# Block 0 with another order of loads, and the spills of the first four filter spectra moved into the down projection

## The chip, the cores and the metric

The kernel runs on one core of a Trainium2 chip. The metric is device time in microseconds of one launch; the median of three runs of the kernel before is 561.41 us (558.75 to 562.42). The profile of the kernel before is of one such run, with a span of 556.9 us from its first to its last instruction. The engines are called as the profile calls them: PE (matmul), DVE (vector), ACT (scalar), POOL (GpSimd) and SP, whose queue issues nearly all the DMA transfers.

## The reference, cut to what matters

A block with conditioning has two halves: a gated long convolution along the sequence, and a gated feed-forward layer. All tensors are bfloat16; S = 2048 rows, D = 576 columns, F = 4608.

```python
mod = (silu(c) @ w_mod).reshape(1, 6, 1, -1)         # w_mod: 576 x 3456
sa, ca, ga, sb, cb, gb = (mod[:, i] for i in range(6))

h = layernorm(q) * (1 + ca) + sa
k_shift = sum over t of k[t - j] * shift_k[:, j]      # 4 taps
kv = k_shift * v
y = irfft(rfft(kv padded) * rfft(ssm_k padded))[:S] + kv * ssm_D
x = q + ga * (h * y)

h2 = layernorm(x) * (1 + cb) + sb
out = x + gb * ((silu(h2 @ w1) * (h2 @ w3)) @ w2)
```

The long convolution is causal: row s of y needs all rows of kv up to s, and the filter ssm_k at the same distances.

## The kernel before

The 2048 rows are cut into eight blocks of 256 rows for the convolution and four groups of 512 rows for the feed-forward layer. Each block s has a spectrum X[s] of its kv rows and a spectrum V[s] of its stretch of the filter (both are 128 x 3456 in bfloat16, 864 KB). Block s of the output is the sum over j of X[j] * V[s-j], so later blocks use earlier spectra again. Only three X and four V fit on chip; the others are written to DRAM (`Xd`, `Vd`) and read back.

The feed-forward layer of group r runs on PE while the convolution of the next two blocks (a Python generator, advanced a little after each piece) uses DVE, ACT and the gaps of PE. A scheduler puts the instructions after block 1 in order, engine by engine; in block 0 the order of PE, DVE and ACT is that of the program text.

The start of the kernel, and block 0:

```python
    def early_loads(self):
        nc = self.nc
        self.crow = self.hp.tile([1, D], BF16, name="crow", tag="sg")
        self.shk_raw = self.prod.tile([1, 4 * D], BF16, name="shk_raw", tag="p")
        nc.scalar.dma_start(self.shk_raw[:], self.shift_k.rearrange("d j -> (d j)").rearrange("(o n) -> o n", o=1))
        def between():
            self.load_k(0)                           # ssm_k, block 0 -> knat
            nc.sync.dma_start(self.crow[:], self.c)
            self.load_x(0)                           # q, block 0
        self.load_kv(0, between)                     # k with its halo -> kh, and v -> vt; one row of kh on ACT's queue
        nc.scalar.dma_start(self.drow[0:4, :], self.ssm_D[0:512].rearrange("(a p) -> a p", p=P))
        nc.scalar.dma_start(self.drow[4:5, 0:64], self.ssm_D[512:D].rearrange("(o p) -> o p", o=1))
        self.load_mod(0, 3)                          # w_mod for sa, ca, ga: 1.9 MB
        self.load_mod(3, 2)                          # w_mod for sb, cb: 1.3 MB

    def first_block(self):
        ...
        self.angles(nc.vector, 1)
        self.whole_turns(1)
        self.whole_turns(0)
        self.shift_taps()                            # PE spreads shift_k over the partitions; ACT, DVE copy it
        self.waves(1)                                # ACT: sine table Fk, for the filter
        self.waves(0)                                # ACT: sine table Fb, for the kv rows
        self.warm(4)                                 # four matmuls without use, to keep PE busy
        ...
        self.cond_silu()
        pt = self.ps((P, 2, 1024), BF16)
        nc.tensor.transpose(pt[:, 0, 0:5], self.drow[:], self.ident[0:5, 0:5])
        nc.scalar.copy(self.dcol[:], pt[:, 0, 0:5])  # ssm_D as a column
        tap = self.knat[:, :, 0]
        nc.gpsimd.tensor_add(tap, tap, self.dcol[:]) # ssm_D is added to the filter's tap 0
        self.run_all(self.k_rows(0))                 # PE transposes knat, ACT copies it: kT
        self.load_k(1)
        self.warm(4)
        rows = self.kv_rows(0)                       # DVE: shifted k times v
        self.cond()                                  # PE, ACT: silu(c) over the partitions: crep
        self.run_all(self.w_spectrum(0))             # PE: 16 matmuls on Fk, ACT: 4 copies -> W
        self.run_all(rows)
        mean, rstd = self.quick_stats(x1[:, 1, :], "l1")
        ...
        self.run_all(self.x_spectrum(0))             # PE: 16 matmuls on Fb, ACT: 4 copies -> X
        self.run_all(self.v_block(0))                # DVE: V from W
        ...                                          # loads of w1, w3; products X*V; mod_piece(2), (1), (0) on crep
        ps = [self.inverse(0, cc) for cc in range(2)]
        self.run_all(self.gate(0))
        self.run_all(self.k_rows(1))
        self.mod_columns()
        pt = [self.ps((P, 2, 1024), BF16) for _ in range(2)]
        self.residual_row(0, 0, ps[0])
        st = [self.quick_stats(x1[:, 0, :], "l2")]
        self.residual_row(0, 1, ps[1])
        self.normed(0, 0, *st[0])
        self.turn_split(pt[0], 0)                    # PE transposes half 0 of h2
        self.turned_split(pt[0], 0, False)           # ACT: five pieces into h2T
        st.append(self.quick_stats(x1[:, 1, :], "l2"))
        self.normed(0, 1, *st[1])
        self.turn_split(pt[1], 1)
        self.turned_split(pt[1], 1, True)            # ACT: three pieces, DVE: two
        ...
```

The spectra and their spills, and the two phases of a group of 512 rows:

```python
    def x_sums(self, s):
        ...
        if 1 < s < NBLK - 2:
            self.keep_x(s)                           # X[s] -> Xd, on SP's queue

    def v_block(self, s):
        ...
        self.V[s] = V
        if 1 < s < NBLK - 1:
            self.keep_v(s)                           # V[s] -> Vd, on SP's queue
        yield 0.75

    def down(self, r, rate):                         # h @ w2
        nc = self.nc
        for h in range(2):
            accs = [self.ps() for _ in range(2)]
            for f0 in range(0, NF, W2C):
                w = self.w2p.tile([P, W2C, H], BF16, name="w2t", tag="w2t")     # 4 buffers
                nc.sync.dma_start(w[:], ...)
                ...
                for f, t in order:
                    nc.tensor.matmul(...)
                self.advance(rate * W2C * 4 * 0.126)

    def row_blocks(self, n1):                        # n1 = 6
        ...
            if r == 0:
                for fc in (n1 - 2, n1 - 1):
                    self.hidden(0, fc, 256, 512, rate, self.kept[fc])
                for fc in range(n1, NF // FC):       # weight pieces 6, 7, 8
                    self.hidden(0, fc, 0, RB, rate)
                    if fc - n1 < 2:
                        self.keep_x(fc - n1)
                        self.keep_v(fc - n1)
                for fc in range(n1 - 2):             # pieces 0 to 3 again, for rows 256 to 511
                    self.hidden(0, fc, 256, 512, rate)
            ...
            self.down(r, rate)
```

A weight piece (`wst`) is 128 columns times 4 of w1 and of w3, 1152 KB in four transfers, and has two buffers. Before this loop, the rows of block 0 alone (256) have gone through pieces 0 to 5 while the convolution of block 1 ran.

Of the kernel before, what the change touches and what calls it, by code (L numbers as in the profile page):

```python
# [9 lines left out]
BF16 = mybir.dt.bfloat16  # L10
# [5 lines left out]
P = 128  # L16
S = 2048
D = 576
F = 4608
B = 256  # L20
NBLK = S // B
# [6 lines left out]
W2C = 4  # L28
# [13 lines left out]
class _Kernel:  # L42
# [28 lines left out]
    def setup(self):  # L71
# [3 lines left out]
        self.npi = const.tile([P, 1], F32, name="npi")  # L75
        self.neghalf = const.tile([P, 2], F32, name="neghalf")
        self.shk = const.tile([P, 4, D], BF16, name="shk")
        self.drow = const.tile([5, P], BF16, name="drow")
        self.dcol = const.tile([P, 5], BF16, name="dcol")
        self.h3 = const.tile([P, NF, RB], BF16, name="h3")  # L80
        self.wm = self.h3[:].rearrange("p a b -> p (a b)")
# [23 lines left out]
        nc.vector.memset(self.neghalf[:], -0.5)  # L105
        self.one = self.small.tile([1, P], BF16, name="one", tag="one", bufs=1)
        nc.vector.memset(self.one[:], 1.0)
        nc.vector.memset(self.drow[:], 0.0)
        self.ang = {}
        self.angles(nc.gpsimd, 0)  # L110
        make_identity(nc, self.ident[:])
# [3 lines left out]
    def early_loads(self):  # L115
        nc = self.nc
        self.crow = self.hp.tile([1, D], BF16, name="crow", tag="sg")
        self.shk_raw = self.prod.tile([1, 4 * D], BF16, name="shk_raw", tag="p")
        nc.scalar.dma_start(self.shk_raw[:], self.shift_k.rearrange("d j -> (d j)").rearrange("(o n) -> o n", o=1))
        def between():  # L120
            self.load_k(0)
            nc.sync.dma_start(self.crow[:], self.c)
            self.load_x(0)
        self.load_kv(0, between)
        nc.scalar.dma_start(self.drow[0:4, :], self.ssm_D[0:512].rearrange("(a p) -> a p", p=P))
        nc.scalar.dma_start(self.drow[4:5, 0:64], self.ssm_D[512:D].rearrange("(o p) -> o p", o=1))
        self.load_mod(0, 3)
        self.load_mod(3, 2)

    def load_mod(self, m, n):  # L130

# [217 lines left out]
    def v_block(self, s):  # L349

        nc = self.nc
        W = self.Wl[s]
        V = self.spec.tile([P, 6, D], BF16, name="V", tag="V")
        if s == 0:
            nc.vector.tensor_copy(V[:, 0:6:3, :], W[:, 0:4:2, :])
            VS = W[:, 1:4:2, :]
        else:
            Wp = self.Wl[s - 1]
            nc.vector.tensor_add(V[:, 0:5:4, :], W[:, 0:4:3, :], Wp[:, 1:3, :])
            nc.vector.tensor_sub(V[:, 1:4:2, :], W[:, 1:3, :], Wp[:, 0:4:3, :])  # L360
            VS = V[:, 1:6:3, :]
        nc.vector.tensor_add(V[:, 2:6:3, :], V[:, 0:6:3, :], VS)
        yield 2.25
        nc.vector.tensor_sub(V[:, 1:6:3, :], VS, V[:, 0:6:3, :])
        self.V[s] = V
        if 1 < s < NBLK - 1:
            self.keep_v(s)
        yield 0.75

# [203 lines left out]
    def first_block(self):  # L573
# [5 lines left out]
        self.whole_turns(1)  # L579
        self.whole_turns(0)  # L580
        self.shift_taps()
        self.waves(1)
        self.waves(0)
        self.warm(4)
        sums = [self.small.tile([P, 1], F32, name="l1" + k, tag="sr" + k) for k in "um"]
        self.cond_silu()

        pt = self.ps((P, 2, 1024), BF16)
        nc.tensor.transpose(pt[:, 0, 0:5], self.drow[:], self.ident[0:5, 0:5])
        nc.scalar.copy(self.dcol[:], pt[:, 0, 0:5])  # L590
        tap = self.knat[:, :, 0]
        nc.gpsimd.tensor_add(tap, tap, self.dcol[:])
        self.run_all(self.k_rows(0))
        self.load_k(1)
        self.warm(4)
        rows = self.kv_rows(0)
        self.cond()
        self.run_all(self.w_spectrum(0))
        self.run_all(rows)
        mean, rstd = self.quick_stats(x1[:, 1, :], "l1")  # L600
        nmr = self.small.tile([P, 1], F32, name="l1nm", tag="nmr1")
# [30 lines left out]
        self.residual_row(0, 0, ps[0])  # L632
        st = [self.quick_stats(x1[:, 0, :], "l2")]
        self.residual_row(0, 1, ps[1])
        self.normed(0, 0, *st[0])
        self.turn_split(pt[0], 0)
        self.turned_split(pt[0], 0, False)
        st.append(self.quick_stats(x1[:, 1, :], "l2"))
        self.normed(0, 1, *st[1])
        self.turn_split(pt[1], 1)  # L640
        self.turned_split(pt[1], 1, True)
        W1 = self.w_spectrum(1)
# [186 lines left out]
    def down(self, r, rate):  # L829
# [4 lines that stand above are left out]
                w = self.w2p.tile([P, W2C, H], BF16, name="w2t", tag="w2t")  # L834
                nc.sync.dma_start(w[:], self.w2[f0 * P:(f0 + W2C) * P, h * H:(h + 1) * H]
                                  .rearrange("(a p) d -> p a d", p=P))
                last = f0 + W2C == NF
                order = [(f, t) for f in range(W2C) for t in range(4)]
                if last:
                    order = [(f, t) for t in range(4) for f in range(W2C)]  # L840
                for f, t in order:
                    nc.tensor.matmul(accs[t // 2][:, t % 2, 0:H],  # L842
                                     self.h3[:, f0 + f, t * P:(t + 1) * P], w[:, f, :],
                                     start=(f0 + f == 0), stop=(f0 + f == NF - 1))
                self.advance(rate * W2C * 4 * 0.126)
            for t in range(4):
                s, cc = 2 * r + t // 2, t % 2
# [32 lines left out]
    def row_blocks(self, n1):  # L880
        for r in range(NRB):
# [7 lines left out]
            if r == 0:  # L889
# [3 lines left out]
                for fc in range(n1, NF // FC):  # L893
                    self.hidden(0, fc, 0, RB, rate)
                    if fc - n1 < 2:
                        self.keep_x(fc - n1)
                        self.keep_v(fc - n1)
                for fc in range(n1 - 2):
                    self.hidden(0, fc, 256, 512, rate)
            else:  # L900
# [57 lines left out]
```

## Time and profile before

| what | number |
|---|---|
| median of three runs | 561.41 us (558.75 to 562.42) |
| span of the profiled run | 556.9 us |
| PE busy | 525.7 us (94%) |
| DVE busy | 316.6 us (57%) |
| ACT busy | 303.8 us (55%) |
| bytes moved by DMA | 119.29 MB, mean 214 GB/s |
| block 0, from 0 to 38.4 us: PE busy | 27.75 us |
| from 84 to 110 us: PE busy, DMA | 26.00 us, 327 GB/s |
| from 110 to 137 us: PE busy, DMA | 23.50 us, 321 GB/s |

PE is the busiest engine by far, so what the time can lose is PE's idle time, and what a change can add is work or waits on PE. Nearly all idle time of PE lies in three places: block 0, the stretch from 119 to 137 us (the end of the hidden phase of the first group) and around 172 us (the end of its down phase). From 190 us on PE stands still only for fractions of a microsecond at a time.

A line of the timeline has the start and the busy time of an instruction or a run of equal ones, the engine (PE; PEld for weight loads; a q after the name for the engine's queue, which issues transfers), the line of the kernel, the operation, the output and inputs, and in square brackets how long the engine had stood idle and what ended that. A line of the windows has the stretch, its length, the busy time and number of instructions of each engine, the granted clock of PE as a share of full speed, the mean busy share of the sixteen DMA engines, and GB/s.

### The profile page before, as it was taken

How to read it: one execution, taken by the hardware profiler on the slowest of the kernel's cores; microseconds unless marked ns; L12 is line 12 of the kernel's file. 1: busy time of each engine (PE TensorE's matmuls, PEld its weight loads, DVE VectorE, ACT ScalarE, POOL GpSimd, SP SyncE). 2: the span in 40 equal slices, each digit the busy share in tenths (PEclk: the TensorE clock that was granted, in tenths of full speed). 3: DMA queues.
4: the chain of work that ended last, by engine and by line, in shares of the span. 5: the costliest groups of instructions: out<-in, count | busy, mean ns of one | idle time of the engine just before them, and what ended most of it. 6: DMA issues, size and time to landing. Idle time of an engine off the chain costs nothing.

```text
span 556.9 us, 9033 instructions
## 1 busy us (share of the span) xinstructions
PE 525.7 (94%) x3495; PEld 305.0 (55%) x3495; DVE 316.6 (57%) x486; ACT 303.8 (55%) x638; POOL 45.5 (8%) x111
## 2 busy tenths in 40 slices
PE   5969989997997999999999999989999999999996
PEld 2656665444775644434477744334478733333775
DVE  8679656696884268595894259979442121222011
ACT  4658686956924166848915165675955055555100
POOL 3202010202102000101101000030201000000000
PEclk9979989998999999999999999999999999999999
DMA  8953689998898677966897679654264545432352
GB/s 246 288 158 110 218 299 298 333 341 263 300 314 267 186 264 228 340 225 197 292 326 250 179 239 353 202 164 153 89 184 123 148 143 167 143 121 77 99 154 88
DMA packets 103206, 119.29 MB, mean 214 GB/s; under 512 B 5179, under 2 KB 93308, under 8 KB 103164
## 3 DMA queue, kind: packets, MB, share of 16 engines
q1 hardware_dynamic: 103150, 118.72, 67.8%
q8 instruction: 27, 0.44, 0.3%
q14 instruction: 15, 0.12, 0.1%
q10 hardware_dynamic: 14, 0.01, 0.0%
HBM read 104.84 MB, written 13.86 MB: 213 GB/s over the span
## 4 chain that ended last, share of the span: by engine, by line
PE 66%; ACT 10%; DVE 10%; DMA 7%; issue 3%; POOL 3%; SPq 0%; ACTq 0%; DVEq 0%
PE ps L801 32%; PE ps L842 19%; PE ps L809 5%; PE ps L288 4%; ACT junk L401 4%; DMA wst<-in_B_w_dram 3%; DVE p L380 3%; DMA X<-Xd 2%; DVE z L382 2%; PE ps L485 2%; ACT h2row L513 1%; ACT sg L815 1%; DMA V<-Vd 1%; ACT X L291 1%; PE ps L518 1%
## 5 line engine op out<-in xcount | busy, mean ns | idle before, releaser
L801 PE MATMUL ps<-h2T,wst 128*128 128x512 bf16 (+1 forms) x1344 | 272.4, 352 | 5.7 <-DMA wst<-in_B_w_dram 4.1
L801 PEld LDWEIGHTS <-wst 128*128 128x128 bf16 x1344 | 126.5, 99 | 133.5 <-issue 24.1
L815 ACT ACTIVATE sg<-ps 128x512 bf16<-128x512 f32 (+1 forms) x168 | 91.3, 543 | 150.0 <-PE ps L809 90.0
L842 PE MATMUL ps<-w2t,h 128*128 128x288 bf16 x1152 | 143.6, 286 | 0.9 <-DMA w2t<-in_B_w_dram 0.8
L842 PEld LDWEIGHTS <-h 128*128 128x128 bf16 x1152 | 112.3, 98 | 29.9 <-DMA w2t<-in_B_w_dram 1.5
L818 DVE TENSOR_TENSOR h<-sg,u 128x512 bf16<-128x512 bf16 (+1 forms) x168 | 63.5, 383 | 110.6 <-ACT u L817 110.3
L817 ACT CAST u<-ps 128x512 bf16<-128x512 f32 (+1 forms) x168 | 88.6, 527 | 0.8 <-DVE h L818 0.8
L850 DVE TENSOR_TENSOR og<-ps,gbrow 128x288 bf16<-128x288 f32 x32 | 13.1, 449 | 82.6 <-PE ps L842 82.6
L380 DVE TENSOR_TENSOR p<-X,V 128x3456 bf16<-128x3456 bf16 x28 | 54.6, 1951 | 4.2 <-DMA X<-Xd 3.9
L382 DVE TENSOR_TENSOR z<-z,p 128x3456 bf16<-128x3456 bf16 x28 | 54.6, 1950 | 0.1
L809 PE MATMUL ps<-h2T,wst 64*128 64x512 bf16 (+1 forms) x336 | 46.7, 352 | 0.5 <-ACT X L291 0.5
L401 ACT ACTIVATE junk<-x 128x576 bf16<-128x576 bf16 x58 | 40.0, 689 | 12.9 <-DVE x L501 12.3
L416 POOL TENSOR_SCALAR l1m<-l1s 128x2 f32<-128x2 f32 x7 | 7.8, 1110 | 241.8 <-ACT junk L401 241.8
L809 PEld LDWEIGHTS <-wst 64*128 64x128 bf16 x336 | 9.8, 94 | 31.9 <-issue 30.6
L288 PE MATMUL ps<-kv,Fb 128*128 128x288 bf16 x128 | 19.5, 291 | 3.8 <-ACT u L817 2.3
L681 ACT CAST y<-ps 128x576 bf16<-128x576 f32 x14 | 8.9, 643 | 22.2 <-PE ps L485 22.2
L288 PE MATMUL ps<-kT,Fk 128*128 128x288 bf16 x128 | 20.8, 316 | 0.0
L513 ACT ACTIVATE h2row<-x,l2n,l2r 128x576 bf16<-128x576 bf16 (+1 forms) x28 | 16.2, 671 | 7.5 <-POOL l2n L421 7.5
L291 ACT CAST W<-ps 128x576 bf16<-128x576 f32 x32 | 19.2, 662 | 1.6 <-PE ps L288 1.5
L291 ACT CAST X<-ps 128x576 bf16<-128x576 f32 x32 | 18.9, 661 | 0.3 <-PE ps L288 0.3
L288 PEld LDWEIGHTS <-Fb 128*128 128x128 bf16 x128 | 12.2, 100 | 12.1 <-issue 6.7
L308 DVE TENSOR_TENSOR kv<-kv,kvt 128x1152 bf16<-128x1152 bf16 x24 | 18.0, 752 | 0.3
(115 smaller groups left out, 327.7 us busy)
## 6 DMA issues: line engine op xcount, KB each, us to landing
wst<-in_B_w_dram SPq DMA_DIRECT2D x80, 512.0 KB, 5.3
w2t<-in_B_w_dram SPq DMA_DIRECT2D x72, 288.0 KB, 3.1
X<-Xd SPq DMA_DIRECT2D x12, 864.0 KB, 7.7
V<-Vd SPq DMA_DIRECT2D x10, 864.0 KB, 8.4
Vd<-V SPq DMA_DIRECT2D x7, 864.0 KB, 4.7
Xd<-X SPq DMA_DIRECT2D x6, 864.0 KB
wst<-in_B_w_dram SPq DMA_DIRECT2D x80, 64.0 KB, 3.6
kh<-in_A_k_dram SPq DMA_DIRECT2D x7, 720.0 KB, 6.1
```

Of the source, the lines that this page charges most:

```text
L288: nc.tensor.matmul(ps[:, h, 0:H], basis[:, cc, cs, e, :], rhs[:, cc, h * H:(h + 1) * H], start=(cc == 0), stop=(cc == 1))
L291: nc.scalar.copy(dst(e, cs).rearrange("p (h d) -> p h d", h=2), ps[:, :, 0:H])
L380: nc.vector.tensor_mul(p[:], X[:], V[:])
L382: nc.vector.tensor_add(z[:], z[:], p[:])
L401: self.nc.scalar.activation(junk[:], src[:, i, :], func, accum_out=out[:, col:col + 1])
L513: self.nc.scalar.activation(row[:, cc, at:at + hi - lo], x1[:, cc, lo:hi], ACT.Identity, bias=b[:, cc:cc + 1], scale=r[:, cc:cc + 1])
L801: nc.tensor.matmul(gus[fi][:, i, 0:n], w[:, 5 * i + ct, fi * P:(fi + 1) * P], hT[:, ct, t0:t1], start=(first and ct == 0), stop=(not first ...
L809: nc.tensor.matmul(gus[fi][:, i, 0:n], w[rows, 4, fi * P:(fi + 1) * P], hT[rows, 4, t0:t1], start=first, stop=not first)
L815: nc.scalar.activation(sg[:, 0:n], gus[fi][:, 0, 0:n], ACT.Silu)
L817: nc.scalar.copy(u[:, 0:n], gus[fi][:, 1, 0:n])
L818: nc.vector.tensor_mul(self.h3[:, f, t0:t1], sg[:, 0:n], u[:, 0:n])
L842: nc.tensor.matmul(accs[t // 2][:, t % 2, 0:H], self.h3[:, f0 + f, t * P:(t + 1) * P], w[:, f, :], start=(f0 + f == 0), stop=(f0 + f == NF ...
```

## The change: what it does and what it is for

Three parts.

The first is block 0. ssm_D is loaded in one transfer at the head of ACT's queue, is turned by two small matmuls right after the taps, and is added to the filter before the sine tables are made; the filter's rows are turned next, and silu(c) and its spreading over the partitions (`cond`) come after them, `cond` after the matmuls of the filter's spectrum. One matmul without use fewer stands ahead of them. The load of w_mod for sb and cb, and the next block's filter, are held back until DVE has done three of the four taps: a one-element write into the destination makes the transfer wait. This is to let the transfers that block 0 needs first go alone, and to take ACT's and PE's work in the order in which the path needs it.

The second is the end of block 0: the statistics of the second half of the rows are taken before the first half is normalised, and DVE takes two of the five pieces of both halves of h2T.

The third moves the spills of V[0] to V[3] out of the hidden phase of the first group into its down phase, four of them spread over the loads of w2.

```diff
@@ setup, early_loads
-        self.drow = const.tile([5, P], BF16, name="drow")
+        self.drow = const.tile([9, 64], BF16, name="drow")
...
-        nc.vector.memset(self.drow[:], 0.0)
+        nc.vector.memset(self.dcol[:], 0.0)
...
+        nc.scalar.dma_start(self.drow[:], self.ssm_D.rearrange("(a p) -> a p", p=64))
         nc.scalar.dma_start(self.shk_raw[:], ...)
...
         self.load_kv(0, between)
-        nc.scalar.dma_start(self.drow[0:4, :], self.ssm_D[0:512].rearrange("(a p) -> a p", p=P))
-        nc.scalar.dma_start(self.drow[4:5, 0:64], self.ssm_D[512:D].rearrange("(o p) -> o p", o=1))
         self.load_mod(0, 3)
-        self.load_mod(3, 2)
@@ v_block
-        if 1 < s < NBLK - 1:
+        if 3 < s < NBLK - 1:
             self.keep_v(s)
@@ first_block
         self.shift_taps()
+        ps = self.ps()
+        nc.tensor.matmul(ps[0:64, 0, 0:5], self.drow[:], self.ident[0:9, 0:9:2], start=True, stop=True)
+        nc.tensor.matmul(ps[64:P, 0, 0:4], self.drow[:], self.ident[0:9, 1:9:2], start=True, stop=True)
+        nc.scalar.copy(self.dcol[:, 0:4], ps[:, 0, 0:4])
+        nc.scalar.copy(self.dcol[0:64, 4:5], ps[0:64, 0, 4:5])
+        tap = self.knat[:, :, 0]
+        nc.gpsimd.tensor_add(tap, tap, self.dcol[:])
         self.waves(1)
         self.waves(0)
-        self.warm(4)
+        self.warm(3)
         sums = ...
+        self.run_all(self.k_rows(0))
         self.cond_silu()
-
-        pt = self.ps((P, 2, 1024), BF16)
-        nc.tensor.transpose(pt[:, 0, 0:5], self.drow[:], self.ident[0:5, 0:5])
-        nc.scalar.copy(self.dcol[:], pt[:, 0, 0:5])
-        tap = self.knat[:, :, 0]
-        nc.gpsimd.tensor_add(tap, tap, self.dcol[:])
-        self.run_all(self.k_rows(0))
-        self.load_k(1)
         self.warm(4)
         rows = self.kv_rows(0)
+        for _ in range(3):
+            next(rows)
+        nc.vector.memset(self.wm[0:1, 3 * D:3 * D + 1], 0.0)
+        self.load_mod(3, 2)
+        self.load_k(1)
+        self.run_all(self.w_spectrum(0))
         self.cond()
-        self.run_all(self.w_spectrum(0))
         self.run_all(rows)
...
         self.residual_row(0, 1, ps[1])
+        st.append(self.quick_stats(x1[:, 1, :], "l2"))
         self.normed(0, 0, *st[0])
         self.turn_split(pt[0], 0)
-        self.turned_split(pt[0], 0, False)
-        st.append(self.quick_stats(x1[:, 1, :], "l2"))
         self.normed(0, 1, *st[1])
+        self.turned_split(pt[0], 0, True)
         self.turn_split(pt[1], 1)
@@ down
                     nc.tensor.matmul(...)
+                if r == 0 and (f0 // W2C) % 4 == 3:
+                    self.keep_v(2 * h + f0 // (4 * W2C))
                 self.advance(rate * W2C * 4 * 0.126)
@@ row_blocks
                     if fc - n1 < 2:
                         self.keep_x(fc - n1)
-                        self.keep_v(fc - n1)
```

The program text says where a spill is meant to stand, but the scheduler orders SP's queue by what is ready. In the built program the four spills stand ahead of the down phase: V[0] and V[1] around the load of weight piece 8, V[2] between the two halves of the next load of piece 0, V[3] after the spill of X[2] and just ahead of the next load of piece 1. The first three loads of w2 stand earlier than before, after the load of piece 7. The readback of V[3] stands where it stood, behind the load of piece 1. On DVE, PE and ACT nothing of note is moved after block 0.

## The prediction

> **What bounds the kernel now.** I read the page's busy times first, then its slices, to see where PE falls short, since PE is busy 94% of the span.
>
> ```profile
> PE 525.7 (94%) x3495; PEld 305.0 (55%) x3495; DVE 316.6 (57%) x486; ACT 303.8 (55%) x638; POOL 45.5 (8%) x111
> ...
> PE   5969989997997999999999999989999999999996
> ...
> DMA  8953689998898677966897679654264545432352
> ```
>
> PE's idle time is 556.9 - 525.7 = 31 us, most of it in the first third; DMA stands at 8 to 9 there too. The windows by stage say how much is at stake where the change acts.
>
> ```profile
> 0.00:38.40 38.40, 27.75 (x196) 17.41 (x197) 28.47 (x58) 20.42 (x37) 9.97 (x27) 0.92 0.88 250
> ...
> 84.00:110.00 26.00, 26.00 (x169) 13.79 (x168) 16.91 (x26) 20.44 (x43) 3.61 (x6) 1.00 0.99 327
> 110.00:137.00 27.00, 23.50 (x163) 13.27 (x161) 24.30 (x34) 16.66 (x42) 2.99 (x6) 0.96 1.01 321
> ```
>
> Block 0 is a chain of single steps, no engine's throughput. From 84 to 137 us the DMA engines are full (shares 0.99 and 1.01) at 321 to 327 GB/s: a byte added there has to be paid. PE feels it only in the second half, where it waits for weights; the timeline of PE has these two:
>
> ```profile
> 124.11 0.61 PE L801 MATMUL ps<-h2T,wst 128*128 128x256 bf16 x4 [0.59 <-DMA wst<-in_B_w_dram]
> ...
> 134.65 0.93 PE L801 MATMUL ps<-h2T,wst 128*128 128x256 bf16 x4 [1.47 <-DMA wst<-in_B_w_dram]
> ```
>
> For block 0 I followed the timeline of all engines:
>
> ```profile
> 5.47 0.23 ACTq L126 DMA_DIRECT2D drow<-in_A_ssm_D_dram  x1
> 5.74 1.29 ACT L182 CAST shk<-ps 128x1024 bf16<-128x1024 f32 x2 [3.74 <-DVE ang L160]
> ...
> 9.80 0.35 POOL L592 TENSOR_TENSOR knat<-knat,dcol 128x5 bf16<-128x5 bf16 x1 [3.87 <-ACT dcol L590]
> ...
> 10.20 1.25 PE L336 MATMUL ps<-ident,knat 128*128 128x128 bf16 x10 [1.90 <-POOL knat L592]
> ...
> 11.49 1.12 ACT L338 COPY kT<-ps 128x1152 bf16<-128x1152 bf16 x1 [1.77 <-PE ps L336]
> ...
> 13.87 4.02 PE L288 MATMUL ps<-kT,Fk 128*128 128x288 bf16 x16
> ```
>
> The filter's matmuls cannot start before 13.87 because the tap waits for ssm_D, and ssm_D for the second of its two transfers, whose issue sits in ACT's stream: ACT stops until 5.47, and only then copies the taps, though PE had begun them at 2.90. Sine tables, silu and the ssm_D copy follow in that order.
>
> **What the Trainium skill says.** "TensorE: Matmul & The Clock Gate", section on the architecture, says ACT and DVE are strict FIFO; the ACT lines above agree: nothing passes the blocked issue. Its part on the HAM clock gate says that a busy window of about 3.4 us, free-running, doubles PE's clock and an idle one halves it. The trace agrees in kind: the 16 filter matmuls take 4.02/16 = 0.25 us each, the later ones of the same width 0.13, and the granted clock falls to 0.5 after PE's pause from 30.7 to 33.5. "DMA: Bandwidth & Descriptors", section on queues, rings and completion order, says descriptors on a ring are consumed in order. I checked that with bytes: from the load of weight piece 6 (issued 82.8) to that of piece 1 (landed 124.1) the queue holds 12.5 MB, which at 326 GB/s is 38.5 us; counted from 84 it ends at 122.5, so landing comes 1.6 us behind. The queue is FIFO to that accuracy.
>
> **Block 0, step by step.** One more issue ahead of the taps' load (0.26 us for the small one, up to 0.5) moves the taps on PE from 2.90 to about 3.4 and their end from 4.97 to 5.4. ACT, no longer blocked, copies the last taps by 5.95 instead of 7.03. Two ssm_D copies of 0.14 to 0.2 us: 6.3. The filter landed at about 6.45, so POOL's add (0.35) ends at 6.85 rather than 10.15. PE is in three idle matmuls of 0.43 us until 7.3, transposes until 8.55 (1.25), and four more idle matmuls until 10.3 (1.7). ACT makes Fk and Fb from 6.3 to 8.5, kT until 9.65. So the filter's matmuls start at 10.3, not 13.87: 3.6 us earlier. They end at 14.3 (4.02), the last W copy at 15.0. Here some is given back: `cond`'s two copies (0.59 + 0.26) now stand on ACT between W and X, so X's copies start at 15.9 against 18.88: 3.0 us. DVE's product chain then starts at 17.05 against 20.09. PE's mod pieces start at about 17.3 rather than 20.16; they need w_mod, whose last part landed at 19.0 in the trace. By 17.8 about 4.4 MB had been moved, while the transfers up to and with the first part of w_mod are 3.6 MB, a sum reached at about 15. With the second part held back I expect landing at 15 to 16.5, just in time. ACT's sums for the layer norm, behind ga, start at 19.5 against 22.24: 2.75 us, and POOL, hg and the residual follow at that distance. I take 2.9.
>
> The end of block 0: the pieces of h2T are ACT 5, ACT 3, DVE 2 before; ACT 3, DVE 2, ACT 3, DVE 2 after. The second half's statistics (0.82 + 0.21 + 0.15 us) move ahead of the first half's normalising (0.63), so the first transposes come 1.3 us later and the second 0.4 earlier, and the last DVE pieces end at 38.6 against 38.5 on the old clock. Worth nothing: 0 to 0.2. Sum for block 0: **-2.9 us** (-1.5 to -4). As PE is full or waits on its own buffers after it, all of it should reach the end.
>
> **The spills.** Each is 864 KB, 0.885 MB, or 2.7 us of the full queue. Before they were issued so:
>
> ```profile
> 71.68 0.43 SPq L389 DMA_DIRECT2D Vd<-V  x1
> ...
> 89.67 0.35 SPq L389 DMA_DIRECT2D Vd<-V  x1
> ...
> 95.75 6.65 SPq L389 DMA_DIRECT2D Vd<-V  x2
> ```
>
> In the built order V[0] moves from 71.7 into the full stretch (+2.7 us). In exchange the next block's k (0.74 MB, 2.3 us) moves out of it: it stood behind piece 6 and now stands ahead, at about 79.4, while DMA is at 0.49 and 0.16 of its time from 80 to 84. Three w2 loads go to about 94. Queue by queue at 326 GB/s on the old clock: piece 6, v and X[1] done at 91.2; piece 7 at 94.4; filter and w2 at 98.2; V[0] 102.2; piece 8 at 105.4; V[1] 108.1; V[2] 111.7; piece 0 at 115.3; X[2] 118.0; V[3] 120.7; piece 1 at 124.4. Landing 1.7 later is 126.1 against 124.07, a wait 2 us longer. But piece 2 is the wait that counts next: readback of V[3], k, v and it end at 133.9, landed 135.8 instead of 134.86. So the two waits are not added: PE is **+1 us** later at 136 (0 to +3). Behind that DMA falls idle in both. The down phase gets no spill, so it doesn't gain; it keeps its own wait on the block's convolution:
>
> ```profile
> 172.41 0.56 PE L518 MATMUL ps<-ident,h2row 128*128 128x128 bf16 x5 [2.00 <-ACT h2row L513]
> ```
>
> That is a chain on DVE behind a readback of X, whose order is unchanged. **Sum:** -2.9 + 1.0 = -1.9 us, or 559.5 from the median; as the four times known (558.6, 558.75, 561.4, 562.4) average 560.3, I say 558.8.
>
> **Rivals.** (1) The full queue is the bound after all: V[0] costs its 2.7 us and the readback of V[3], which must now wait for its own spill, blocks SP and all weights behind it. For it: shares of 1.0 for 52 us. Against: k moves out, and V[3] lands at about 122.4, before the next k would be issued (123.7) anyway. Time: 561 to 563. (2) w_mod becomes the wait of block 0: held to 19.0, PE's mod pieces gain 1 us instead of 2.9, and the time is 560.5. Against: 0.8 MB leaves the queue ahead of it. (3) PE's clock rises one window earlier, as the idle matmuls now run without a pause into the filter's: up to 2 us more in the filter's and X's matmuls, though copies of 0.64 us a group then bind. Time: 557.
>
> **Range and chances.** Run to run the kernel spreads over 3.7 us; block 0 is uncertain by 1.3, the spills by 1.5. Together: 555.5 to 562.3. Two percent are 11 us, more than all the idle time of block 0, so faster by that has 0.02; slower 0.02, if weights are blocked repeatedly; 0.96 within.
>
> **What would show it.** Right: ACT's taps at 4.2 without the queue's block, the first filter matmul at 10.3, hidden matmuls from 35.5 instead of 38.4, the waits on weights near 121 to 133 one or two us longer. Wrong: mod pieces waiting for w_mod; SP blocked at V[3]'s readback beyond 124; new waits of PE between 84 and 119.

## The result, and the profile after

The changed kernel takes 554.64 us (median of four runs, 553.28 to 554.84) against 560.33 us of the kernel before beside it (558.75 to 562.42): a ratio of 0.9891, 95% interval 0.985 to 0.9932. Twenty more runs of the same program in a later series gave 556.5 us (551.18 to 561.61) against 560.15 us, a ratio of 0.9925 [0.9898, 0.9953]. The change is worth about 4 us, perhaps somewhat more, and the first four runs lay on the lucky side of its spread. I had predicted 558.8 us and a range from 555.5 to 562.3; the first measurement fell below it by 0.9 us, while the median of the twenty later runs lies inside it.

The page of the changed kernel: its busy times, then its slices.

```profile
PE 520.8 (94%) x3495; PEld 302.5 (55%) x3495; DVE 317.3 (57%) x489; ACT 302.9 (55%) x637; POOL 46.8 (8%) x111
...
PE   6888899997988999999998999989899999999996
...
PEclk9969999999999999999999999999999999999999
DMA  8935789998996686976996689553364535432452
```

And the clock's line from the page of the kernel before, which was not shown yet:

```profile
PEclk9979989998999999999999999999999999999999
```

The span fell by 4.0 us (556.9 to 552.9), and PE's busy time fell by 4.9 us (525.7 to 520.8) with the same number of matmuls, 3495. PE's idle time, which the change was to shorten and which I had counted, did not fall over the whole span: 31.2 to 32.1 us. Equal work took PE less time, and the clock's lines say how: before, slices 3, 6 and 10 are below full speed, after, only slice 3. The later two of before need not be the change's doing: the second profile of the changed kernel has slices of this kind as well.

The windows put most of this in block 0. Each stretch ends with the first hidden matmul of its kernel. The columns are those of the windows of before: stretch, length, busy time and count of PE, then of its weight loads, DVE, ACT and POOL, the granted clock, DMA's share, GB/s. Before:

```profile
0.00:38.40 38.40, 27.75 (x196) 17.41 (x197) 28.47 (x58) 20.42 (x37) 9.97 (x27) 0.92 0.88 250
```

After:

```profile
0.00:33.53 33.53, 24.48 (x196) 16.23 (x197) 28.79 (x60) 19.29 (x36) 10.73 (x27) 0.89 0.93 287
...
84.00:110.00 26.00, 26.00 (x155) 12.42 (x154) 18.16 (x27) 20.30 (x41) 3.61 (x6) 1.00 1.01 332
110.00:137.00 27.00, 23.29 (x179) 14.66 (x178) 21.10 (x31) 18.14 (x51) 4.80 (x12) 1.00 0.91 305
```

The hidden matmuls start 4.87 us earlier. The same 196 matmuls were busy 3.27 us less (27.75 - 24.48), and PE's idle time fell by 1.60 us (10.65 to 9.05). From 84 to 110 us PE is as full as before (26.00 us), so no new waits arose there. The granted clock in this view can't be read for the first microseconds: it shows full speed until its first recorded event, at 18.7 us before and 9.1 us after, though the matmuls ahead of it run at half speed. The durations of equal matmuls are the safer reading. The timeline of the changed kernel, with start and busy time first:

```profile
0.75 0.60 ACTq L119 DMA_DIRECT2D drow<-in_A_ssm_D_dram  x1
...
4.95 1.44 ACT L180 CAST shk<-ps 128x1024 bf16<-128x1024 f32 x2 [2.95 <-PE ps L173]
...
6.29 0.17 ACT L584 CAST dcol<-ps 128x4 bf16<-128x4 f32 x1
...
6.81 0.21 POOL L587 TENSOR_TENSOR knat<-knat,dcol 128x5 bf16<-128x5 bf16 x1 [0.94 <-DMA knat<-in_A_ssm_k_dram]
...
7.31 1.27 PE L334 MATMUL ps<-ident,knat 128*128 128x128 bf16 x10
8.38 1.40 PE L569 MATMUL ps<-h2T,ident 128*128 128x512 bf16 x4
9.79 2.12 PE L286 MATMUL ps<-kT,Fk 128*128 128x288 bf16 x16
...
12.56 0.76 DVE L308 TENSOR_TENSOR kv<-kv,vt 128x1152 bf16<-128x1152 bf16 x1
...
13.09 0.29 ACT L199 CAST crep<-ps 64x128 bf16<-64x128 f32 x1
...
13.37 1.83 PEld L286 LDWEIGHTS <-Fb 128*128 128x128 bf16 x16 [1.10 <-DVE kv L308]
13.37 2.13 PE L286 MATMUL ps<-kv,Fb 128*128 128x288 bf16 x16 [0.96 <-ACT crep L199]
15.34 4.36 PE L208 MATMUL ps<-h,crep 128*128 128x288 bf16 x30
```

The two lines of the kernel before that answer to the last two, from the same view:

```profile
17.68 2.65 PE L288 MATMUL ps<-kv,Fb 128*128 128x288 bf16 x16
20.16 4.36 PE L210 MATMUL ps<-h,crep 128*128 128x288 bf16 x30
```

The chain of ssm_D is as planned: the add waits for the filter's own load and nothing else, and the modulation's matmuls (L208) wait for no load of w_mod. The sixteen filter matmuls, however, take 2.12 us and not 4.02: PE ran them at the full clock. Not all of that is won: X's matmuls, next on PE but for `cond`, wait 0.96 us. Their line names ACT's copy of `crep`, but that copy ends at 13.38, after they have begun; the weight load beside them names DVE's product kv, which ends at 13.32, and the second profile of the changed kernel names kv for the matmuls too (0.85 us). So DVE is what X waits for once the filter's matmuls are fast.

The waits on weight pieces at the end of the first hidden phase, after:

```profile
120.20 0.61 PE L806 MATMUL ps<-h2T,wst 128*128 128x256 bf16 x4 [0.78 <-DMA wst<-in_B_w_dram]
...
127.33 0.61 PE L806 MATMUL ps<-h2T,wst 128*128 128x256 bf16 x4 [1.07 <-DMA wst<-in_B_w_dram]
...
130.20 0.61 PE L806 MATMUL ps<-h2T,wst 128*128 128x256 bf16 x4 [1.29 <-DMA wst<-in_B_w_dram]
```

They fall about 4 us earlier than the three of before (124.11, 131.61, 134.65), and their sum is 3.1 us against 3.5. The prediction showed two of those three and left out the one between them:

```profile
131.61 0.61 PE L801 MATMUL ps<-h2T,wst 128*128 128x256 bf16 x4 [1.44 <-ACT junk L401]
```

The profile puts it down to ACT, but the weights of these matmuls landed at 131.56, just as that ACT instruction ended, and a second profile of the same kernel has this wait at 131.43, put down to the weights.

The moved spills were issued so:

```profile
94.21 0.49 SPq L387 DMA_DIRECT2D Vd<-V  x1
...
97.30 0.66 SPq L387 DMA_DIRECT2D Vd<-V  x1
...
103.85 0.54 SPq L387 DMA_DIRECT2D Vd<-V  x1
...
109.51 1.47 SPq L387 DMA_DIRECT2D Vd<-V  x1
...
116.54 0.34 SPq L392 DMA_DIRECT2D V<-Vd  x1
```

The last spill landed at 116.47, and the readback of the same spectrum went out at 116.54. SP's queue stood for 0.9 us ahead of it, so nothing was blocked for long.

### The profile page after: what moved, and what is told of

It reads as the page before. It is cut to its first block, busy times and chain, and to the rows that moved or that the text cites. A ratio compares the mean times of both kernels' runs of the same rounds, so it can differ in the third digit from the quotient of the medians.

```text
span 552.9 us, 9038 instructions
## 1 busy us (share of the span) xinstructions
PE 520.8 (94%) x3495; PEld 302.5 (55%) x3495; DVE 317.3 (57%) x489; ACT 302.9 (55%) x637; POOL 46.8 (8%) x111
## 4 chain that ended last, share of the span: by engine, by line
PE 64%; ACT 11%; DVE 10%; DMA 8%; issue 3%; POOL 3%; SPq 0%; DVEq 0%; ACTq 0%
PE ps L806 31%; PE ps L847 19%; PE ps L814 5%; DMA wst<-in_B_w_dram 4%; ACT junk L399 4%; PE ps L286 4%; DVE p L378 3%; DMA X<-Xd 2%; DVE z L380 2%; PE ps L483 2%; ACT h2row L511 2%; ACT sg L820 1%; DMA V<-Vd 1%; ACT u L822 1%; ACT X L289 1%
## 5 line engine op out<-in xcount | busy, mean ns | idle before, releaser
L847 PEld LDWEIGHTS <-h 128*128 128x128 bf16 x1152 | 112.3, 98 | 31.2 <-DMA w2t<-in_B_w_dram 2.8
L399 ACT ACTIVATE junk<-x 128x576 bf16<-128x576 bf16 x58 | 40.1, 692 | 13.2 <-DVE x L499 12.6
L305 DVE TENSOR_TENSOR kvt<-kh,shk 128x1152 bf16<-128x1152 bf16 x24 | 18.1, 755 | 2.1 <-DMA kh<-in_A_k_dram 2.0
L286 PE MATMUL ps<-kT,Fk 128*128 128x288 bf16 x128 | 19.1, 299 | 0.0
```

Source lines behind the costliest of these rows:

```text
L286: nc.tensor.matmul(ps[:, h, 0:H], basis[:, cc, cs, e, :], rhs[:, cc, h * H:(h + 1) * H], start=(cc == 0), stop=(cc == 1))
L399: self.nc.scalar.activation(junk[:], src[:, i, :], func, accum_out=out[:, col:col + 1])
L847: nc.tensor.matmul(accs[t // 2][:, t % 2, 0:H], self.h3[:, f0 + f, t * P:(t + 1) * P], w[:, f, :], start=(f0 + f == 0), stop=(f0 + f == NF ...
```

## The experiments

Theory: the gain is block 0's, and what I had left out of it is PE's clock, which rises earlier because PE works on without a pause. Rivals: the moved spills carry part of the gain; the held-back loads do; the new end of block 0 does. In the text a spread after a difference of means is one standard error; an interval after a ratio is 95%. The ratios, and the figures of the spread near the end, leave out runs that the comparison marks as disturbed, so that a ratio can differ from that of the two medians.

**Block 0 alone** (the changed kernel with its spills back where they were):

```diff
-        if 3 < s < NBLK - 1:
+        if 1 < s < NBLK - 1:
             self.keep_v(s)
-                if r == 0 and (f0 // W2C) % 4 == 3:
-                    self.keep_v(2 * h + f0 // (4 * W2C))
+                        self.keep_v(fc - n1)         # in the hidden phase, as before
```

> Both changes to block 0, the four spills of V where they stood before. Theory A (the whole 5.7 us come from block 0: its shorter chain, and PE's clock in it): the time stays at 554.6, within 1 us. Rival B (the spills bring about 1.7 us, as the profile after gains from 4.0 to 5.7 us between 127 and 144 us): 556.3. My prediction's own step, that the spills cost 1 us: 553.6.

Measured: 555.87 us (555.12 to 558.1), ratio 0.991 [0.9885, 0.9935]. That is the whole gain within the noise, without the spills.

**The spills alone** (block 0 as before), in two series:

```diff
-        if 1 < s < NBLK - 1:
+        if 3 < s < NBLK - 1:
             self.keep_v(s)
+                if r == 0 and (f0 // W2C) % 4 == 3:
+                    self.keep_v(2 * h + f0 // (4 * W2C))
-                        self.keep_v(fc - n1)
```

> The kernel before with only the spills of V moved. Theory A: 560.3, within 1 us. Rival B: 558.6, with the two weight waits between 119 and 137 us shorter in sum than the 0.59 and 1.47 us of before, or PE's clock not halved at about 135. The prediction's step: 561.3.

Measured: 557.95 us (552.85 to 562.94), ratio 0.9913 [0.9874, 0.9952], which rests on four of its seven runs; the mean of all seven is 1.8 +- 1.4 us below that of before. That looks like a part of the gain, but the profiled execution shows a block 0 that differs from the kernel before although not an instruction in it was changed:

```profile
13.39 2.13 PE L288 MATMUL ps<-kT,Fk 128*128 128x288 bf16 x16
15.37 2.12 PE L288 MATMUL ps<-kv,Fb 128*128 128x288 bf16 x16
```

The filter matmuls ran at the full clock here (2.13 us instead of 4.02), and the hidden matmuls began at 35.82. So I ran it again, and with it the kernel before.

> The moved spills alone on the block 0 of before, once more, because the first set of runs left their effect at -1.5 +- 1.4 us around a mean. Theory (block 0 and the clock carry the gain, the spills nothing): median within 0.7 us of before, ratio 0.999 to 1.002. Rival (the spills carry part): 1.5 to 2.5 us faster, ratio 0.9955 to 0.997. What the prediction said: 1 us slower, ratio 1.002.

Measured: 558.68 us (553.02 to 562.77), ratio 0.9989 [0.9958, 1.0019]; the mean of its fourteen runs is 1.4 +- 0.8 us below before's. Its waits on weights, to be held against 124.11 [0.59] of before:

```profile
123.58 0.61 PE L801 MATMUL ps<-h2T,wst 128*128 128x256 bf16 x4 [0.97 <-DMA wst<-in_B_w_dram]
...
125.10 0.61 PE L801 MATMUL ps<-h2T,wst 128*128 128x256 bf16 x4 [0.91 <-DMA wst<-in_B_w_dram]
...
131.66 0.61 PE L801 MATMUL ps<-h2T,wst 128*128 128x256 bf16 x4 [0.51 <-DMA wst<-in_B_w_dram]
...
133.76 0.61 PE L801 MATMUL ps<-h2T,wst 128*128 128x256 bf16 x4 [0.52 <-DMA wst<-in_B_w_dram]
```

The first wait grew by 1.3 us (0.97 + 0.91 against 0.59), the later ones shrank from 2.9 to 1.0 us. Piece 1 landed at 125.06 (before 124.07), piece 2 at 133.97 (134.86). The spills cost at one wait what they give back at the next. Whether they bring a microsecond in the end, these two series leave open, but a loss of a microsecond fits neither mean well (-1.8 +- 1.4 and -1.4 +- 0.8); beside the new block 0 they bring nothing that can be seen (0.991 without them, 0.9925 with them).

**The kernel before, once more**, for a second profile:

> The kernel before, unchanged, for a second profile of it. If the phase of PE's granted clock is a matter of chance from execution to execution, the hidden layer's first matmul need not fall at 38.4 us as in the first profile: 35.8 to 38.4, with the rise of the clock anywhere from 13 to 19 us, and the time's median at the before's own, ratio 1.00. If that profile's 38.4 is the rule for this program, it comes back within 0.3 us.

Measured: 559.37 us (556.55 to 567.83), ratio 0.9996 [0.9965, 1.0026]. The filter's matmuls again took 4.02 us, and the hidden matmuls began at 38.22:

```profile
13.80 4.02 PE L288 MATMUL ps<-kT,Fk 128*128 128x288 bf16 x16
17.61 2.52 PE L288 MATMUL ps<-kv,Fb 128*128 128x288 bf16 x16
```

My expectation that the phase moves from profile to profile held only in part. With this block 0 the clock's first rise stands at 18.7, 18.4 and 18.0 us in three profiles and at 13.2 in the fourth, the first of the spills alone.

**PE's pause filled in the kernel before**, nothing else changed:

```diff
         nc.scalar.copy(self.dcol[:], pt[:, 0, 0:5])
+        self.warm(5)
         tap = self.knat[:, :, 0]
```

> The kernel before with five more idle matmuls where PE stood still from 8.3 to 10.2 us. Theory (the pause kept the clock at half until 18.7): the clock rises at 9 to 14, the sixteen filter matmuls take 2.1 to 3 us instead of 4.0, and the time falls by 1 to 2 us to about 559. Rival (only the chain of ACT and POOL counts): 560.8, no change.

Measured: 558.57 us (554.47 to 561.33), ratio 0.997 [0.9945, 0.9994]. This is the cleanest view of the clock:

```profile
7.96 2.31 PE L571 MATMUL ps<-h2T,ident 128*128 128x512 bf16 x5
10.07 1.04 PE L336 MATMUL ps<-ident,knat 128*128 128x128 bf16 x10
10.95 1.03 PE L571 MATMUL ps<-h2T,ident 128*128 128x512 bf16 x4
11.90 0.56 PE L198 MATMUL ps<-one,sc 1*128 1x128 bf16 x5
12.40 2.13 PE L288 MATMUL ps<-kT,Fk 128*128 128x288 bf16 x16
14.37 2.12 PE L288 MATMUL ps<-kv,Fb 128*128 128x288 bf16 x16
```

The same two lines in the kernel before, between its transposes and its filter matmuls:

```profile
11.24 1.91 PE L571 MATMUL ps<-h2T,ident 128*128 128x512 bf16 x4
13.09 0.84 PE L198 MATMUL ps<-one,sc 1*128 1x128 bf16 x5
```

The transposes begin at 10.07, nearly as before (10.20): the chain of waits up to them is hardly touched. But the clock rises at 10.7. The idle matmuls and those of `cond`, which stand on PE ahead of the filter's, take 1.59 us instead of 2.75, so that the filter's begin 1.47 us earlier, and these take 2.13 us. The tap was thus not all that held the filter in the kernel before: PE's own idle matmuls at half clock did too. The hidden matmuls begin at 34.82. Five matmuls without use moved block 0's end by 3.6 us in this profile, and the time by 1.7 us in the runs (0.3 to 3.1, from the interval). In the profiled execution the whole lead is gone at the first matmul of the down phase (147.06 us, 146.65 in the first profile of before). From the first hidden matmul to there the same 762 matmuls were busy 103.12 us instead of 100.56, with the clock halved at the start, from 58.5 to 61.9 and from 133.6 to 140.4 us (before: at the start, from 73.4 to 76.8 and from 134.8 to 138.2), and PE stood idle 1.4 us longer. What brought this execution the longer halving isn't settled.

**The new block 0 without its idle matmuls:**

```diff
         self.waves(0)
-        self.warm(3)
         ...
         self.cond_silu()
-        self.warm(4)
```

> The changed kernel without its seven idle matmuls of block 0. Theory: the clock rises at 15 to 18 instead of 9, the filter matmuls take 4.0 us instead of 2.1 and X's up to 2.6, and 2 us are lost: 556.6. Rival (the chain): within 0.5 us of the changed kernel, as transposes and kT do not depend on them.

Measured: 557.0 us (555.26 to 559.17, and one run of the 22 at 2965.56 us, which stays unexplained), ratio 0.9945 [0.9923, 0.9967].

```profile
7.57 1.25 PE L334 MATMUL ps<-ident,knat 128*128 128x128 bf16 x10 [0.73 <-POOL knat L587]
10.35 3.53 PE L286 MATMUL ps<-kT,Fk 128*128 128x288 bf16 x16 [1.54 <-ACT kT L336]
...
14.31 2.13 PE L286 MATMUL ps<-kv,Fb 128*128 128x288 bf16 x16
```

Here PE pauses again, the clock rises at 13.3, the filter's matmuls take 3.53 us, and the hidden matmuls begin at 34.70. The change without these matmuls gives 3.1 us of time (1.8 to 4.3, from the interval), the pause filled in the old order 1.7 us (0.3 to 3.1), the whole change about 4.2 us (2.6 to 5.7). They add up to within their errors. But beside the changed kernel in the same series this one is slower by only 0.5 us in the medians and 0.7 +- 0.6 us in the means (the one run left out). The profile shows the clock at work here; the time is too coarse to tell the 2 us of my theory from the rival's half a microsecond, though it speaks for less than 2. The profiles say why it can be less: with the filter's matmuls at full clock X's wait for kv, so that 3.53 instead of 2.12 us for the filter moves the start of X's from 13.37 to 14.31 only.

**Loads as early as before** (the second part of w_mod and the next filter not held back):

```diff
         self.load_mod(0, 3)
+        self.load_mod(3, 2)
...
         self.cond_silu()
+        self.load_k(1)
...
-        nc.vector.memset(self.wm[0:1, 3 * D:3 * D + 1], 0.0)
-        self.load_mod(3, 2)
-        self.load_k(1)
```

> The changed kernel with the second part of w_mod and the next filter loaded early as before, with no write that holds them. Theory (held back, the first part of w_mod lands in time for the mod pieces, which begin at 15.3): without it the first part lands at 17.8 to 19, the mod pieces wait 2.5 to 3.5 us, and the time is 557 to 558. Rival (the queue is in order, what stands behind does not matter): 554.6 and no wait.

Measured: 555.32 us (553.22 to 556.47), ratio 0.9887 [0.9863, 0.9911]. The modulation's matmuls start without a wait:

```profile
15.31 4.36 PE L209 MATMUL ps<-h,crep 128*128 128x288 bf16 x30
```

My theory of a wait of 2.5 to 3.5 us was wrong. Holding the loads back brings nothing: w_mod was not what ended last.

**ssm_D's one load back behind the loads of k and v:**

```diff
-        nc.scalar.dma_start(self.drow[:], self.ssm_D.rearrange("(a p) -> a p", p=64))
         nc.scalar.dma_start(self.shk_raw[:], ...)
         ...
         self.load_kv(0, between)
+        nc.scalar.dma_start(self.drow[:], self.ssm_D.rearrange("(a p) -> a p", p=64))
```

> The changed kernel with the one load of ssm_D moved back behind ACT's load of k and v, where the first of the two stood before. Theory (what stopped ACT until 5.47 us was the issue of the second transfer; one transfer anywhere in the queue is enough): ACT copies the taps at or before 4.95 us, POOL's add of ssm_D stays at 6.8 to 7.1, the filter's matmuls start at 9.8 to 10.3, and the time is the changed kernel's, ratio to before 0.990 to 0.993. Rival (the place in the queue is what counts): the issue blocks ACT until about 5.4, the taps are copied from 5.7, ssm_D's copies come at 7.1, the filter's matmuls start at 10.9 to 11.5 and the time is 0.7 to 1 us longer, ratio 0.993 to 0.995.

Measured: 555.16 us (552.62 to 561.01), ratio 0.9923 [0.99, 0.9946].

```profile
2.23 0.32 ACTq L125 DMA_DIRECT2D drow<-in_A_ssm_D_dram  x1
...
3.22 1.44 ACT L180 CAST shk<-ps 128x1024 bf16<-128x1024 f32 x2 [1.22 <-PE ps L173]
...
6.41 0.16 ACT L584 CAST dcol<-ps 128x4 bf16<-128x4 f32 x1 [1.75 <-PE ps L583]
...
6.71 0.76 POOL L587 TENSOR_TENSOR knat<-knat,dcol 128x5 bf16<-128x5 bf16 x1 [0.84 <-ACT dcol L585]
...
10.04 2.12 PE L286 MATMUL ps<-kT,Fk 128*128 128x288 bf16 x16
```

The issue no longer stops ACT at that place, which copies the taps from 3.22. What had stopped it until 5.47 was the second of the two transfers. The trace of the kernel before names what that issue waited for: the first eight transfers of the program each count their completion on a semaphore of their own, and this later one shares the semaphore of SP's second load of k (issued at 1.17) and carries a wait on it. The last signal of that load came at 5.45 us and the issue at 5.47; with PE's pause filled it was 5.16 and 5.18. In the changed kernel, and here, all of ACT's loads ahead of the taps are among the first eight, and none carries this wait. So it was not the size of the transfer that stopped ACT, but the landing of another. The place at the head of the queue brings no time, and in the profile it costs some: with the load moved back the taps' matmuls begin at 2.17 us instead of 3.91, DVE's product kv ends at 12.81 instead of 13.32, and X's matmuls begin at 12.87 and the hidden ones at 33.01, earlier than in any other profile here, though the filter's begin 0.25 us later. The joining of two transfers into one does the work.

**Without the new end of block 0:**

```diff
-        st.append(self.quick_stats(x1[:, 1, :], "l2"))
         self.normed(0, 0, *st[0])
         self.turn_split(pt[0], 0)
+        self.turned_split(pt[0], 0, False)
+        st.append(self.quick_stats(x1[:, 1, :], "l2"))
         self.normed(0, 1, *st[1])
-        self.turned_split(pt[0], 0, True)
```

> The changed kernel with the end of block 0 (statistics, normalising, pieces of h2T) as before. The prediction's step (worth 0 to 0.2 us): 554.7. Rival (the end is where the start of the hidden phase gained from 4.1 to 4.9 us): 555.4.

Measured: 556.99 us (553.86 to 562.71), ratio 0.994 [0.992, 0.9961], about 0.8 us behind the changed kernel's 0.9925, with intervals that overlap. From the first modulation matmul to the first hidden one this kernel takes 18.47 us (15.57 to 34.04), the changed one 18.19 and 18.08 in its two profiles. That is no measure of the new end: the same stretch takes 18.1 to 18.5 us in the five profiles with the old block 0, and 18.4 in two others that have the new end (block 0 alone, and without idle matmuls). What the new end is worth isn't told apart by these runs.

**The changed kernel again, and its clock kept up through the modulation.** PE does 60 matmuls of one column at 23.1 us, and in the changed kernel the clock is halved at 26.2. Twelve idle matmuls of 448 columns among them:

```diff
                     nc.tensor.matmul(out, w5[0:k, ct, m * D + lo:m * D + lo + n],
                                      self.crep[0:k, ct, 0:1], start=(ct == 0), stop=(ct == 4))
+                nc.tensor.matmul(ps[:, i, 64:512], self.ident[:], self.h2T[0][:, 0, 0:448], start=True, stop=True)
```

> The changed kernel once more, beside the others on one chip, as its four runs are few against a kernel before that spread from 555.65 to 563.23. If the spread of the parts is chance: 555 to 556, so that without the new end (557.0) and without the moved spills (555.9) it loses 1 to 2 us each. If the four runs were typical: 554.6.

> The changed kernel with twelve idle matmuls of 448 columns among the sixty one-column matmuls of the second modulation, which stand where PE's clock is halved at 25.7 to 28.3 us in every profile. Theory (PE's clock is a good part of what the change gained, and of the spread): no halving until the hidden phase, filter and hidden matmuls from 31.6 to 36.4 at full speed, time 1.5 to 2 us below the changed kernel, and less spread. Rival (the end of block 0 is bound by DVE and ACT): no gain, or 0.5 us lost to the added matmuls.

Measured: the changed kernel 556.5 us, as told above; with the idle matmuls 555.36 us (553.04 to 559.26), ratio 0.9921 [0.9884, 0.9958] beside 0.9925. The halving moved to 31.9 us and the hidden matmuls began at 33.11 (33.53 and 33.86 without), but the time shows no difference; the 1.5 to 2 us of my theory did not come.

The second profile of the changed kernel has a span of 555.9 us, 3.0 us above the first, and the windows show where most of that arose:

```profile
110.00:137.00 27.00, 22.74 (x158) 13.26 (x156) 20.01 (x29) 16.08 (x44) 2.90 (x8) 0.87 0.84 278
```

The same stretch of the same program had a clock of 1.00 in the first profile. PE waits for weights here, and in this execution the clock was halved from 129.5 to 136.3 us, so that PE got through 158 recorded matmuls instead of 179. The first matmul of the down phase came at 143.18 instead of 140.94 us, although PE had been 0.5 us ahead at 114.

**Early loads and kept clock together**, as the best version that the runs suggested (the edits of the two experiments above, both on the changed kernel):

> The changed kernel with w_mod's second part loaded early again and idle matmuls between the one-column matmuls of the modulation. Each alone was within 1 us of the changed kernel. If both are nothing, the median is 555.5 to 556.5, ratio to before 0.992 to 0.993. If each gives its 0.7 us, 554.5 to 555, ratio 0.990.

Measured: 553.82 us (551.53 to 557.96), ratio 0.9908 [0.9871, 0.9945]. It beats the kernel before; against the changed kernel the intervals overlap, so I can't say that it is better. Its hidden matmuls began at 34.27 us, later than in either profile of the changed kernel.

## Why the prediction was wrong

**The chain of ssm_D: right.** Tap add predicted to end at 6.85, ended at 7.02; transposes until 8.55, ended at 8.58; kT until 9.65, ended at 9.74; filter matmuls from 10.3, began at 9.79, as the four idle matmuls ahead of them took 1.40 us and not 1.7. Only the taps came later than I said (first matmul at 3.91 instead of 3.4). They were not on the path to the filter's matmuls, but DVE's product kv begins with them, and X's matmuls waited for kv. That the second queue issue stops ACT is shown by the run with one late load; what it waited for, the landing of a load of k, I had not seen.

**"They end at 14.3 (4.02)": wrong, and the step that failed.** I kept the half-clock duration of the filter matmuls. They took 2.12 us, and 2.12 to 3.08 in the seven other profiles with the new order and its idle matmuls. From there on everything came about 2 us ahead of my times: X's matmuls, the modulation (15.34 instead of 17.3), ACT's sums (17.42 instead of 19.5) and the hidden matmuls (33.53 instead of 35.5). Block 0 gave -4.9 us in the first pair of profiles where I had -2.9. Without the idle matmuls, where the filter's took 3.53 us, it gave -3.5 to -3.7 (34.70 against 38.22 and 38.40): the steps of the chain were about right, and the term mis-sized was the duration of PE's work. The third rival had named this, with "up to 2 us more" and a time of 557, and I gave it no share of the central number. The sign in its favour was in my own working, which had PE in idle matmuls and transposes without a pause until 10.3. What I set against it, that copies of 0.64 us a group would bind, was true (ACT's four copies of W take 2.27 us) and no contradiction: they bind at 2.3 us, well below 4.02.

The Trainium skill supports this reading. "TensorE: Matmul & The Clock Gate", section "What's actually happening", says that the window in which PE's activity is counted runs freely, and that the number of matmuls at the half clock therefore varies from run to run of one kernel. The trace agrees: with the old block 0 the first rise stood at 18.7, 18.4, 18.0 and 13.2 us; with PE's pause filled, at 10.7; with the new order and its idle matmuls, at 9.1 to 12.1 in all eight profiles; without the idle matmuls, at 13.3. So with the pause of 1.9 us ahead of the transposes the rise came some 7 to 8 us later in three profiles of four, and 2.4 us later in the fourth, than in the one profile with the pause filled. As the window runs freely, part of each such difference is chance; one profile can't divide it, and it is the 22 runs with the pause filled that show a gain.

**The give-back by `cond`: wrong in kind.** I had 0.6 us of delay by ACT's two copies of `crep`. ACT itself stood idle for 0.70 us after them until X's first matmuls were done, and these had waited 0.96 us for DVE's kv, a wait that my steps did not have.

**w_mod, the second rival: excluded.** There was no wait for it, held back or not.

**The end of block 0: not resolved.** 0 to 0.2 us predicted; about 0.8 us in the ratios with intervals that overlap, and nothing in the profiles that stands out of their spread.

**"Spills +1 us": not confirmed.** The queue arithmetic was good for the first wait (piece 1 one microsecond later with the spills alone; I had two), and wrong for the second: I had piece 2 landing 1 us later, and it came 0.9 us earlier. The ratio of the first series of the spills alone leaves no room for a loss, but rests on four runs; that of the second reaches from 2.4 us gained to 1.1 us lost. Both means lie on the side of a gain. In the changed kernel the question shifts anyway, because PE frees its buffers 4 us earlier and the whole stretch, spills and loads, moves forward with it; my sum had held the queue's end at a fixed hour. The first rival, a full queue that holds up the weights, falls: the readback of V[3] went out 0.07 us after the spill landed, and the waits in this stretch sum to 3.1 us, less than before.

**The range: too narrow for what one execution does.** I took the spread of four runs, 3.7 us. The 140 runs of the kernel before that count in the four series reach from 555.35 to 563.67 us, with a standard deviation of 2.1 us. The mean of four such runs is uncertain by 2.1 / 2, about 1 us, even for a perfect prediction of the average. My estimate for the miss of 4.2 us (558.8 to 554.64) is 2.0 us of block 0's clock, taken from the profiles, 1.0 us for the spills that cost nothing, and some 1.2 us of luck in the four runs; the twenty later runs are slower by 1.9 us. This division isn't shown: the run without idle matmuls finds only about half to one microsecond of time for the clock that they keep.

**Where the spread comes from.** Over those 140 runs the time falls by 3.6 us for each percent of mean granted clock (correlation -0.57, so that 32% of the variance goes with it). In the profiles, behind block 0, the clock is halved for 3.4 or 6.8 us at a time, beginning at 57 to 73, 129 to 135 or 166 to 172 us in one profile or another, and not in every execution: the first profile of the changed kernel has none between 36.4 us and its end, the second has two. What makes the other 68% of the variance is open.

## What to carry to other kernels

In a chain of short steps at the start of a kernel, ask for every pause of PE whether it holds the clock down for the matmuls behind it; here a pause of 1.9 us cost 1.7 us (0.3 to 3.1) on top of its own length, and five matmuls without use took that back. Ask the same of matmuls without use that stand in the path: at half clock four of them took 1.91 us and held the filter's. And where an engine's queue stops at a small transfer, ask which semaphore its issue waits on, before its size or its place is blamed. When a plan moves matmuls earlier, work out their duration again for the clock they will meet, and give the rival who says so a share of the number. Before a range is put round a change of 1%, look at how far single executions lie apart: twenty runs were needed here to see 4 us of 560 to within 1.5.

## What the runs showed that I had not expected

Matmuls of one column do not keep the clock up. In the changed kernel PE works from 23.10 to 26.99 on 60 of them with no gap of note, and the clock is halved at 26.2; in its other profile at 27.1. With twelve matmuls of 448 columns among them the halving came at 31.9 and, in the combined version, at 30.7. The prediction had put the halving of before down to PE's pause from 30.7 to 33.5 us; there too the sixty matmuls stand ahead of it, from 26.98 to 30.71, and the clock was halved at 32.4, inside the pause. Whether the later halving is worth anything isn't shown: the first hidden matmul came 0.4 to 0.8 us earlier in one profile with these matmuls (33.11), but at 34.27 in the combined version and at 33.01 in the changed kernel with ssm_D's load moved back, which has none of them. A single profile can weigh little here.

Idle time and gain can also part ways: over the whole span PE stood idle 0.9 us longer in the changed kernel and still ended 4.0 us earlier.
